# Top-k attention and SwiGLU FFN: a floor under the FFN pieces of even turns, and a slightly smaller share for the others

## The chip, the cores and the metric

The kernel runs on one core of a Trainium2 chip. The metric is the device time of one execution in microseconds; the time before is the median of three runs. The core's engines work through their own instruction queues in order: TensorE (PE in the profile, its weight loads PEld), VectorE (DVE), ScalarE (ACT), GpSimd (POOL), and SyncE (SP), whose queue issues nearly all of the transfers.

## What is computed

Attention with 8 batches, 8 heads, 576 positions and 64 numbers a head, in float32. Of each row of scores only the 32 largest count. The result, as 4608 tokens of 512 numbers, goes through a SwiGLU feed-forward network (FFN) with an inner width of 1536.

```python
scores = scale * np.matmul(q, k.transpose(0, 1, 3, 2))
kth = np.partition(scores, -top_k, axis=-1)[..., -top_k:-top_k + 1]
scores = np.where(scores >= kth, scores, -1000000000.0)
attn = np.exp(scores - np.max(scores, axis=-1, keepdims=True))
attn = attn / (np.sum(attn, axis=-1, keepdims=True) + 1e-09)
x = np.matmul(attn, v)               # then (B,H,S,D) -> (B*S, H*D)
g = x @ w_gate
out = (g * (1.0 / (1.0 + np.exp(-g))) * (x @ w_val)) @ w_out
```

## The kernel before

**Units.** Attention is cut into 160 units. A batch has 20 of them: five tiles of queries (`qt` 0 to 4), each for four pairs of heads (`hp` 0 to 3). The first four tiles have 128 queries and two heads each: full units. The fifth has the last 64 queries, and a unit of it holds both heads in one set of 128 rows, so it has one row block to select from instead of two: a short unit. Units 16 to 19 of every batch are short, so are units 36 to 39, 56 to 59, and so on.

**What a unit goes through.** `scores` multiplies queries and keys on PE into PSUM banks of the ring `ps_t` (five banks), and ACT copies them to `sc` (L314 for short units, L329 for full ones). `select` finds the 32 largest on DVE with four rounds of MAX8 (L346) and three of MATCH_REPLACE8 (L350). `shift` makes a bias on POOL (L361). `weigh` applies Prelu (L373) and Exp (L378) on ACT. `normalize` adds and inverts the sum on DVE (L391, L392) and scales `e`: from unit 12 on the first head on ACT (L396), the second, where there is one, on POOL (L398). `turn` transposes `e` on PE (`etps`, L411; nine transposes for a full unit, five for a short one) into banks of the same ring, and ACT copies them to `et` (L412). `values` multiplies with `v` on PE (`av`, L447), and ACT copies the result to `xT` (L463). `prep` transposes the keys and queries of the next batch on PE (`kqps`, L263 and L270), during the short turns and the first turn behind them.

**Turns.** The main loop runs over turns n. Turn n selects in unit n, weighs and scales unit n - 1, and transposes unit n - 2. Even turns also have the values of units n - 4 and n - 3 and the scores of units n + 1 and n + 2; odd turns have neither. (The scores of two short units are made together.) The order within a turn is written out by hand, and every engine keeps it, because at the end of the program each instruction is tied behind the one before it on its engine:

```python
        if nxt and (n < 2 or len(nxt) > 1):
            run(nxt.pop(0))          # scores of unit n + 1
        if valued(n):
            finish_units(valued(n))  # values
        ...                          # scores of unit n + 2, weigh(n - 1)
        pieces(2)
        flush(on_act)
        ...
            run(turn(n - TURN))      # transposes
        ...
        pieces(1)
        pieces(1)
        run(norm)
        ...
        pieces(6)
```

**Pieces.** The FFN runs over 18 blocks of 256 tokens. `feed` is a generator for one block, cut into pieces for PE. The first half of a block has 24 pieces of four matmuls (L591, tile `f`), each of a cost of 1 credit: two pieces fill a bank with a gate, two with a value, and each bank is then read by ACT (L624 to L626, or L631) and multiplied on POOL (L627, L632). The second half has seven quarters (L657, tiles `y_ps` and `x_ps`) of two pieces each, of 0.75 credit. It multiplies with sums and differences of weights and of halves of the block, which POOL makes (L664, L672, L677, L705); POOL also adds the results up (L644). The quarters run in the order i = 1, 7, 5, 6, 2, 4, 3. A block can start when attention has completed its tokens.

**Credit.** `share(n)` says how many credits a turn gets: 5.8 (turns below 32) or 6.4 (from turn 32 on, `AHEAD`) for a full unit and half of that for a short one, less what PE has else to do in the turn (0.7 for each unit of values and of scores, 0.6 for the transposes, half for short units, and 0.6 where keys and queries are prepared). In the loop, `credit[0] = min(credit[0] + share(n), share(n) + 1)`, and a call of `pieces(k)` takes up to k pieces while the credit is 1 or more. In the last four turns and the three behind them the credit is set to 8. What is left of the FFN comes behind the loop. The credit and the order decide only where a piece stands, not how many there are.

Of the kernel before, what the change touches and what calls it, by code (L numbers as in the profile page):

```python
# [25 lines left out]
def kernel(  # L26
# [49 lines left out]
    AHEAD = 8 * NHP  # L76
# [203 lines left out]
    units = [(b, qt, hp) for b in range(B) for qt in range(J + 1) for hp in range(NHP)]  # L280
    state = {}

    def n_heads(qt):

        return 1 if qt == J else 2
# [514 lines left out]
    def share(n):  # L800


        others = 0.0
        for m, cost in [(m, 0.7) for m in valued(n)] + [(n - TURN, 0.6)]:
            if m >= 0:
                others += cost * (0.5 if units[m][1] == J else 1)
        others += 0.7 * len(scored(n))
        if units[n + 3][1] == 0:
            others += 0.6

        beside = 5.8 if n < AHEAD else 6.4
        return beside * n_heads(units[n][1]) / 2 - others

    def scored(n):

        ahead = [n + 1] if n < 2 else [] if n % 2 else [n + 1, n + 2]
        return [m for m in ahead if m < NU and (units[m][1] < J or m % 2 == 0)]

    def valued(n):

        behind = [] if n % 2 else [n - 4, n - 3]
        return [m for m in behind if 0 <= m < NU]
# [33 lines left out]
    for n in range(NU + 3):  # L856
# [15 lines left out]
        if n >= NU - NHP:  # L872
            credit[0] = 8.0
        else:
            credit[0] = min(credit[0] + share(n), share(n) + 1)
# [93 lines left out]
```

## Time and profile before

| what | value |
|---|---|
| median of three runs | 1743.95 us (1743.23 to 1744.68) |
| the profiled execution's own time | 1745.19 us |
| its span, first to last instruction | 1743.4 us |
| mean granted TensorE clock | 0.970 |
| a full even and odd turn together, 507.6 to 530.0 us | 22.40 us |
| end of the last selection on DVE | about 1655 us |

A row of a group names the line of the kernel, the engine, the operation and the tiles (written, then read). A row of waits reads: engine, line and tile that waited, then after the arrow the engine, line and tile that released it, the total in us, how often, and the longest. In a timeline the first two numbers are start and length in us, and a bracket at the end holds the idle time of the engine just before the row and what ended it. The ends of matmuls are modelled, so the start of one to the start of the next is the better measure of PE's pace.

### The profile page before, as it was taken

What the parts mean: (1) busy time and instruction counts of PE and PEld (TensorE: products, weight loads), DVE (VectorE), ACT (ScalarE), POOL (GpSimd) and SP (SyncE); (2) the same over time, 40 slices, a digit from 0 to 9 for tenths busy, and PEclk for the clock granted to TensorE, in tenths of its full rate; (3) what the DMA queues carried; (4) which work ended last, traced back from release to release, by engine and by line L of the source; (5) the groups of instructions that cost most, each with busy time, mean ns of one, the idle gap of its engine ahead of it and who ended that gap; (6) DMA issues with size and microseconds to landing.
All of it is one profiled execution on the core that took longest, in us unless ns stands there. A gap on an engine that the chain in (4) does not pass through costs nothing.

```text
span 1743.4 us, 31763 instructions
## 1 busy us (share of the span) xinstructions
PE 1661.9 (95%) x11408; PEld 1399.7 (80%) x11408; DVE 1476.0 (85%) x3311; ACT 1259.9 (72%) x2901; POOL 798.4 (46%) x914
## 2 busy tenths in 40 slices
PE   5678999999999999999999999999999999999999
PEld 3468598788888788887888888888888878888887
DVE  6999898999989799898999898898988978898300
ACT  7899787778767686767776777778777767676531
POOL 4798454343353425352535334443444433535334
PEclk6698999999999999999999999999999999999999
DMA  7442030003000120002100030000300020000000
GB/s 204 138 121 86 23 76 2 13 3 82 15 13 1 29 70 1 13 12 60 28 14 1 14 71 27 1 13 20 78 2 13 1 57 15 13 1 13 1 13 12
DMA packets 109309, 59.72 MB, mean 34 GB/s; under 512 B 88544, under 2 KB 96992, under 8 KB 109152
## 3 DMA queue, kind: packets, MB, share of 16 engines
q1 hardware_dynamic: 108016, 57.37, 12.6%
q8 instruction: 90, 1.47, 0.4%
q14 instruction: 67, 0.55, 0.1%
q10 hardware_dynamic: 1136, 0.33, 0.1%
HBM read 48.23 MB, written 9.44 MB: 33 GB/s over the span
## 4 chain that ended last, share of the span: by engine, by line
PE 82%; DVE 7%; ACT 6%; POOL 2%; issue 1%; SPq 1%; DMA 0%; ACTq 0%; POOLq 0%
PE f L591 38%; PE av L447 9%; PE x_ps L657 9%; PE s L324 7%; PE etps L411 7%; PE y_ps L657 6%; DVE m L346 3%; DVE e L350 3%; PE f L507 2%; ACT e L378 2%; PE kqps L270 1%; PE o_ps L559 1%; DVE size L123 1%; ACT e L373 1%; POOL p L644 1%
## 5 line engine op out<-in xcount | busy, mean ns | idle before, releaser
L346 DVE MAX8 m<-e 128x8 f32<-128x576 f32 x864 | 614.6, 747 | 3.1
L350 DVE MATCH_REPLACE8 e<-m,e 128x576 f32<-128x576 f32 x576 | 423.6, 742 | 0.0
L591 PE MATMUL f<-xT,wg 128*128 128x256 f32 x1536 | 356.2, 382 | 0.0
L591 PE MATMUL f<-xT,wv 128*128 128x256 f32 x1536 | 355.2, 381 | 0.0
L591 PEld LDWEIGHTS f<-xT,wg 128*128 128x128 f32 x1536 | 288.5, 191 | 46.5 <-issue 8.8
L591 PEld LDWEIGHTS f<-xT,wv 128*128 128x128 f32 x1536 | 287.4, 190 | 42.9 <-issue 5.5
L627 POOL TENSOR_TENSOR h<-h,half_g 128x512 f32<-128x512 f32 x96 | 122.4, 1275 | 355.5 <-ACT h L626 339.6
L378 ACT ACTIVATE e<-e,bias 128x576 f32<-128x576 f32 x288 | 221.6, 779 | 37.3 <-POOL bias L361 34.3
L411 PE MATMUL etps<-ident,e 128*128 128x128 f32 x1312 | 183.5, 280 | 57.3 <-POOL e L398 25.0
L411 PEld LDWEIGHTS etps<-ident,e 128*128 128x128 f32 x1312 | 154.9, 143 | 86.6 <-POOL e L398 31.2
L373 ACT ACTIVATE e<-sc,m 128x576 f32<-128x576 f32 x288 | 212.4, 792 | 0.0
L350 DVE MATCH_REPLACE8 e<-m,sc 128x576 f32<-128x576 f32 x288 | 211.8, 742 | 0.0
L346 DVE MAX8 m<-sc 128x8 f32<-128x576 f32 x288 | 203.2, 742 | 7.0 <-ACT sc L329 7.0
L329 ACT ACTIVATE sc<-s 128x288 f32<-128x288 f32 x512 | 167.8, 418 | 53.8 <-PE s L324 53.4
L632 POOL TENSOR_TENSOR h<-h,val 128x512 f32<-128x512 f32 x96 | 122.4, 1275 | 173.4 <-ACT val L631 163.2
L398 POOL TENSOR_TENSOR e<-e,tot 128x576 f32<-128x576 f32 x140 | 160.6, 1151 | 81.5 <-DVE tot L392 72.2
L412 ACT COPY et<-etps 128x512 f32<-128x512 f32 (+1 forms) x448 | 184.6, 493 | 15.4 <-PE etps L411 14.9
L324 PE MATMUL s<-kqT 64*128 64x288 f32 x1024 | 172.5, 447 | 12.5 <-ACT et L412 5.9
L391 DVE TENSOR_SCALAR tot<-tot 128x1 f32<-128x1 f32 x228 | 29.3, 145 | 161.6 <-ACT e L378 161.5
L447 PE MATMUL av<-et,v 128*64 128x128 f32 (+1 forms) x2560 | 158.9, 268 | 0.0
L396 ACT ACTIVATE e<-e,tot 128x576 f32<-128x576 f32 x148 | 119.5, 807 | 49.3 <-DVE tot L392 48.9
L447 PEld LDWEIGHTS av<-et,v 128*64 128x64 f32 x2560 | 138.8, 141 | 5.9 <-issue 3.0
(86 smaller groups left out, 2216.8 us busy)
## 6 DMA issues: line engine op xcount, KB each, us to landing
v<-in_v_dram SPq DMA_DIRECT2D x32, 256.0 KB, 3.3
kq_in<-in_k_dram SPq DMA_DIRECT2D x63, 128.0 KB, 2.9
kq_in<-in_q_dram SPq DMA_DIRECT2D x63, 128.0 KB, 3.2
w<-in_moe_w_gate_dram SPq DMA_DIRECT2D x12, 512.0 KB, 3.8
w<-in_moe_w_val_dram SPq DMA_DIRECT2D x12, 512.0 KB, 3.7
w<-in_moe_w_out_dram SPq DMA_DIRECT2D x12, 512.0 KB, 3.6
out_dram<-o SPq DMA_DIRECT2D x38, 128.0 KB, 2.4
out_dram<-o SPq DMA_DIRECT2D x16, 256.0 KB, 2.4
```

Of the source, the lines that this page charges most:

```text
L324: nc.tensor.matmul(ps[:, 0:half], slab[d, q0 : q0 + P], slab[d, k0 : k0 + half])
L329: nc.scalar.mul(sc[:, i * half : (i + 1) * half], ps[:, 0:half], scale)
L346: nc.vector.max(m[:, t, 8 * r : 8 * r + 8], cur[:, hs])
L350: nc.vector.match_replace(e[:, hs], m[:, t, 8 * r : 8 * r + 8], cur[:, from_[t]], LOWEST)
L373: nc.scalar.activation(e[:, hs], sc[:, at], AF.Prelu, bias=m[:, t, TOP_K - 1 : TOP_K], scale=-1.0, alpha=SMALL,)
L378: nc.scalar.activation(e[:, hs], e[:, hs], AF.Exp, bias=bias[:, t : t + 1], scale=-1.0 / SMALL, accum_out=tot[:, t : t + 1],)
L398: nc.gpsimd.tensor_tensor(e[:, hs], e[:, hs], tot[:, t : t + 1].to_broadcast([P, S]), ALU.mult)
L411: nc.tensor.transpose(ps[:, c * P : (c + 1) * P], e[:, k0 : k0 + P], ident[:])
L412: nc.scalar.copy(et[:, c0 : c0 + cn, :], ps[:, 0 : cn * P].rearrange("p (c j) -> p c j", c=cn),)
L447: nc.tensor.matmul(av[d, i, 0:ql], weights_, moving, start=c == (0 if last else J), stop=c == (J if last else J - 1),)
L591: nc.tensor.matmul(ps[:, i, :], w[:, kc, m * P : (m + 1) * P], x[:, kc, :], start=(kc == 0), stop=(kc == KC - 1),)
L657: nc.tensor.matmul(ps, lhsT, T[i][m], start=m == 0, stop=m == MQ - 1)
```

## The change

From turn 32 on, `share` starts from 6.25 instead of 6.4 credits (3.125 instead of 3.2 for a short unit), and in even turns it returns no less than 2.0. The only even turns whose share lay below 2.0 are those of short units. Since `pieces(2)` is the first call in a turn, behind the scores and the values and ahead of the transposes, two pieces can then stand there in such turns.

```diff
         if units[n + 3][1] == 0:
             others += 0.6

-        beside = 5.8 if n < AHEAD else 6.4
-        return beside * n_heads(units[n][1]) / 2 - others
+        beside = 5.8 if n < AHEAD else 6.25
+        least = 2.0 if n >= AHEAD and n % 2 == 0 else 0.0
+        return max(least, beside * n_heads(units[n][1]) / 2 - others)
```

## The prediction

> **What bounds the kernel now.** I read the page from the top: busy shares, the chain of work that ended last, and then, for the part of the span that the change can reach (after 330 us), the waits of PE and a stretch of two pairs of full turns.
>
> ```profile
> span 1743.4 us, 31763 instructions
> PE 1661.9 (95%) x11408; PEld 1399.7 (80%) x11408; DVE 1476.0 (85%) x3311; ACT 1259.9 (72%) x2901; POOL 798.4 (46%) x914
> ...
> PE 82%; DVE 7%; ACT 6%; POOL 2%; issue 1%; SPq 1%; DMA 0%; ACTq 0%; POOLq 0%
> ```
>
> PE carries 82% of the chain. The windows view asks whether that holds in the steady part; its columns are the window, its length, then busy us of PE, PEld, DVE, ACT, POOL, the granted clock, DMA share and GB/s:
>
> ```profile
> 507.60:530.00 22.40, 22.40 (x148) 19.03 (x147) 20.91 (x49) 17.41 (x41) 7.66 (x8) 1.00 0.11 25
> 530.00:552.40 22.40, 22.40 (x148) 19.03 (x147) 20.04 (x47) 16.94 (x38) 8.93 (x9) 1.00 0.01 1
> ```
>
> An even and an odd full turn take 22.40 us, PE is busy in all of it, and DVE has 1.5 to 2.4 us to spare. So a full pair is bound by PE, and the whole time is PE's work plus PE's pauses. PE's waits from 330 to 1700 us:
>
> ```profile
> PE etps L411 <- ACT sc L314: 7.4, 6, 2.0
> PE etps L411 <- POOL e L398: 6.5, 4, 3.4
> PE etps L411 <- ACT e L396: 2.6, 1, 2.6
> PE etps L411 <- ACT sc L329: 2.5, 3, 1.1
> PE s L324 <- ACT et L412: 0.3, 1, 0.3
> ```
>
> Only 19 us of pauses are left, all but 0.3 at the transposes (etps). The two rows with sc, 9.9 us in nine places, are all in even turns of short units (turns 36, 56, 58, 76, 96, 98, 116, 118, 136). One of them, turn 56, in PE's timeline:
>
> ```profile
> 590.76 1.20 PE L307 MATMUL s<-kqT 64*64 64x288 f32 x16
> 591.89 0.66 PE L411 MATMUL etps<-ident,e 128*128 128x128 f32 x4
> 594.54 0.87 PE L411 MATMUL etps<-ident,e 128*128 128x128 f32 x5 [1.99 <-ACT sc L314]
> 595.24 2.72 PE L657 MATMUL x_ps<-wo,h 128*128 128x256 f32 x6
> ```
>
> The fifth transpose opens a second PSUM bank of the ring of five (ps_t). That bank still holds scores, and ACT copies scores out only behind the Prelu and Exp of the unit before (594.00 us). No FFN piece stands between the scores and the transposes, because the turn's credit is below 1.
>
> The POOL row is four odd turns (129, 137, 147, 155). In the worst, POOL's scaling of e for the second head stood behind an FFN block's sums:
>
> ```profile
> 1408.99 1.29 POOL L644 TENSOR_TENSOR p<-p,p 128x512 f32<-128x512 f32 x1
> 1410.21 2.11 POOL L705 TENSOR_TENSOR h<-h,xT 128x256 f32<-128x256 f32 x3
> 1412.26 1.17 POOL L398 TENSOR_TENSOR e<-e,tot 128x576 f32<-128x576 f32 x1
> ```
>
> **What a pause costs.** More than its length. The piece of turn 96 between two sets of transposes (nine transposes and f x16) takes 6.81 us with a pause of 2.00; at the rates of undisturbed turns (0.109 us a transpose, 0.216 an f instruction) it is 4.44. So a pause costs about 0.37 us above its modelled length. And the clock drops behind some:
>
> ```profile
> 595.30:598.70 3.40, 3.40 (x10) 2.66 (x10) 3.20 (x7) 3.31 (x8) 0.67 (x2) 0.50 0.02 5
> 800.10:803.40 3.30, 3.30 (x9) 2.60 (x9) 3.10 (x7) 3.21 (x8) 0.36 (x2) 0.50 0.00 0
> 1001.00:1004.40 3.40, 1.41 (x10) 1.15 (x9) 1.76 (x6) 3.40 (x12) 1.15 (x1) 1.00 0.00 0
> 1414.50:1417.80 3.30, 3.30 (x27) 2.94 (x27) 3.09 (x8) 3.30 (x9) 0.92 (x2) 0.50 0.18 41
> ```
>
> Behind the pauses at 592.55 (1.99 us), 797.01 (2.00) and 1410.07 (3.41) the granted clock is 0.50 for about 3.4 us, a loss of 1.7 us of PE each; behind the one at 1001.14 (2.00) it stays 1.00. The Trainium skill ("TensorE: Matmul & The Clock Gate", HAM oscillation) has the rule that PE must have no idle gap over about 3.4 us. By it only the third would lose clock, and my sum would be 3.4 us smaller. The rows show two losses behind 2 us, so I count three.
>
> **The change, part by part.** A piece is four matmuls, eight PE instructions in the trace, 8 x 0.216 = 1.73 us; in the second half of a block it is six of them, 1.30 us, and costs 0.75 of credit. A block is 24 + 14 x 0.75 = 34.5 credits.
>
> *Short even turns.* The share was 3.2 - 1.4 - 0.6 - 0.7 = 0.5 in the first and 0.2 in the third short turn; it becomes 2.0. Carrying share and credit through turn by turn, the first group of pieces, ahead of the transposes, got 0 or 1 in the twelve such turns from 36 to 138 and now gets 2 in every one; four of them also get a third piece behind the transposes. Two pieces are 2.6 to 3.46 us. The bank comes free 2.6 us after the last score matmul (591.9 to 594.5), so they just cover the wait. Of the first short turns, 36, 116 and 136, which already had one piece, pause 0.28 to 0.62 us; 56, 76 and 96, which had none, pause 2.0. Removed: 9.93 us of pauses, nine times 0.37 = 3.3, and two clock losses, 3.4: **16.6 us**.
>
> *What moves with a piece.* Every second piece brings ACT the reading of its bank, 0.60 + 0.60 + 0.64 us for a gate (L624 to L626) or 0.59 for a value (L631), and POOL a product of 1.28. These now stand ahead of the copies of et on ACT, so those, the kqT copies and the scaling of e for the next turn come later. In turn 58 of before the scaling ended 3.42 us behind the last transpose and was needed at 4.79; with a gate ahead it is about 4.6 against 4.4 to 4.8. I take 0.5 us in each of six odd short turns: **+3 us** (bounds 0, and +11 if the 1.83 us of a gate fell in full on all six). The loads of k and q on SP (L228, L233) wait for the transposes of kq_in, which come up to 5 us later, and stores queue behind them; the next use of such a tile is two turns, some 15 us, later, and a load lands in about 3 us: nothing. If that cover went, 3 us a batch.
>
> *Other turns.* 6.25 for 6.4 takes 0.15 credit from each full turn and 0.075 from an odd short one. A full pair has 8.5 credits for 8.8, so 22.40 - 0.3 x 1.73 = 21.88 us on PE, still above DVE's 20.04 to 20.91. Per batch of 20 turns the share goes from 76.8 to 77.56. PE's total is unchanged; what is done earlier is missing later.
>
> *Where blocks fall.* A block took 34.5 / 3.84 = 8.98 turns and takes 34.5 / 3.878 = 8.90; one is completed by attention every 160 / 18 = 8.89. So blocks used to drift against the turns and now keep step. The POOL burst above starts with a block's fifth quarter (i = 2). Carried through, that quarter started ahead of POOL's scaling in an even turn with full units in blocks 9, 12, 13, 14 and 15 (turns 102, 128, 136, 146, 154): the last four are the four waits. With the change it starts in an odd turn in every block from 3 to 15 but 11, whose turn 118 scales one head, on ACT. Behind an odd turn the next transposes are some 8 us off. Removed: 6.48 us, four times 0.37 = 1.5, one clock loss 1.7: **9.7 us**. What newly falls into even turns is the third quarter with its three subtractions (L677, 3 x 0.73); in turn 54 of before that put POOL's end 3.56 us behind the last transpose, needed at 4.4 at the least: nothing.
>
> *The tail.* By turn 158 three credits more are done, so turn 159 has 3.75 instead of 6.75 and the last unit's chain starts 5.2 us nearer. Its selection had then been waiting 12.65 us (DVE L391 at 1674.81), so it is not late. 30 pieces remain behind the loop as before, and the 2.62 us pause at 1673.5 stays.
>
> Sum: 16.6 + 9.7 - 3 = 23.3 us. The profiled execution took 1745.19 us (span 1743.4 and 1.8 around it), 1.24 above the median; 1745.19 - 23.3 - 1.24 = **1720.6 us**.
>
> **The rivals.**
>
> *Waits of POOL stay or come elsewhere.* Keeping step is as good or bad as the phase it keeps. If another burst meets the scaling, only the short turns gain: 1743.95 - 16.6 + 3 = 1730. Against: the phases above; for: margins of about 1 us at the third quarter.
>
> *DVE binds the full turns: slower.* The skill's page "Perfetto Trace Analysis" (Identifying the Most-Contended Engine) says that [...]weight loads tell the headroom. By these PE is at 19.03 / 22.40 = 85%, and DVE with 20.91 would be the bound. Then the smaller shares give nothing back, while the short turns pay 3.3 credits x 1.73 = 5.7 us a batch against 2.8 of removed waits: 6 x 2.9 = 17 slower, 5.2 back in the tail, 1756. It decides once a pair of DVE needs over 21.88 us. Against: PE's instructions follow at 0.216 us with no pause and DVE idles about 2.3 us in most even turns, so I take the row, not the rule.
>
> *The wait only moves.* Two pieces end and ACT, with the pieces' own reading, is late for the next transposes by as much: 1743 to 1741. The +11 us bound above is half of it. That the change does not do what it says is excluded by the credits: all twelve turns get their two.
>
> **How the numbers follow.** About 0.2%, 3.5 us, can be told from no change. Both kinds of wait go: 0.60 (1716 to 1725). Only the short turns' go: 0.22 (1725 to 1733). Gain smaller but over 3.5 us: 0.05. Within 0.2%: 0.05. Slower: 0.08. The range 1715 to 1733 leaves out the last three and a little of the first.
>
> **What would show it.** Right: no PE wait on ACT sc at etps after 330 us, POOL e at most 2 us, the granted clock at 0.50 nowhere between 330 and 1600 us, full pairs of 21.4 to 22.4 us with PE full, PE's busy time down by the clock losses. Wrong: waits PE etps on ACT e L396 or POOL e of over 5 us, DVE without idle time in even turns, or PE pauses before turn 160.

## The result, and the profile after

The changed kernel takes 1724.4 us (median of four runs, 1721.19 to 1724.58) where the kernel before takes 1743.59 (four runs): 0.9885 of it, with a 95% interval of 0.9868 to 0.9902. That is 19.2 us less; 23.3 were forecast, and 1724.4 lies in the range given. The profiled executions stand at 1724.45 and 1745.19 us.

The page of the changed kernel, with the lines that match those shown of before:

```profile
span 1722.7 us, 31765 instructions
PE 1654.3 (96%) x11408; PEld 1396.9 (81%) x11408; DVE 1476.5 (86%) x3311; ACT 1261.0 (73%) x2901; POOL 799.1 (46%) x914
...
PE 86%; DVE 6%; ACT 5%; issue 1%; POOL 1%; SPq 1%; DMA 1%; ACTq 0%; POOLq 0%
```

The same number of matmuls fills more of a shorter span. Who PE waited for from 330 to 1700 us (waited, released by, total us, times, longest):

```profile
PE etps L411 <- ACT e L396: 2.6, 1, 2.6
PE s L324 <- ACT et L412: 1.9, 5, 0.7
```

The rows on ACT sc (9.9 us before) and on POOL e (6.5) are gone. The one pause of the tail stays, and one row has grown: scores that wait for the copy of et, five times instead of once. Turn 56, the one shown of before, on PE:

```profile
589.80 1.20 PE L307 MATMUL s<-kqT 64*64 64x288 f32 x16
590.93 1.56 PE L657 MATMUL x_ps<-wo,h 128*128 128x256 f32 x6
592.33 1.89 PE L591 MATMUL f<-xT,wg 128*128 128x256 f32 x8
594.05 1.15 PE L411 MATMUL etps<-ident,e 128*128 128x128 f32 x9
```

Two pieces stand between the scores and the transposes, and the nine transposes run in one go, with no bracket for idle time behind them. A pair of full turns is bound by PE as before: two stretches of 22.40 us have PE full and leave DVE 1.9 and 2.4 us.

```profile
510.00:532.40 22.40, 22.40 (x148) 19.03 (x147) 20.48 (x47) 17.11 (x38) 8.19 (x9) 1.00 0.11 25
532.40:554.80 22.40, 22.40 (x148) 19.03 (x147) 20.04 (x47) 16.85 (x40) 7.96 (x9) 1.00 0.00 1
```

Where the time went, between the first transposes of turns 34, 156 and 160 in the two traces:

| stretch | before | after | difference |
|---|---|---|---|
| start to turn 34 | 374.16 | 374.26 | +0.1 |
| turn 34 to 156 | 1242.38 | 1225.44 | -16.9 |
| turn 156 to 160 | 56.22 | 51.04 | -5.2 |
| turn 160 to the end | 70.64 | 71.92 | +1.3 |

The changed kernel does three credits' worth of pieces, 5.2 us, more before turn 156 and as much less behind it. So the pauses between turns 34 and 156 shrank by 16.9 + 5.2 = 22.1 us.

### The profile page after: what moved, and what is told of

Same layout as the page of the kernel before. It is cut to its first block, busy times and chain, and to the rows that moved or that the text cites. A ratio compares the mean times of both kernels' runs of the same rounds, so it can differ in the third digit from the quotient of the medians.

```text
span 1722.7 us, 31765 instructions
## 1 busy us (share of the span) xinstructions
PE 1654.3 (96%) x11408; PEld 1396.9 (81%) x11408; DVE 1476.5 (86%) x3311; ACT 1261.0 (73%) x2901; POOL 799.1 (46%) x914
## 4 chain that ended last, share of the span: by engine, by line
PE 86%; DVE 6%; ACT 5%; issue 1%; POOL 1%; SPq 1%; DMA 1%; ACTq 0%; POOLq 0%
PE f L591 38%; PE x_ps L657 10%; PE av L447 9%; PE s L324 8%; PE y_ps L657 7%; PE etps L411 7%; PE f L507 3%; DVE m L346 3%; DVE e L350 2%; ACT e L378 1%; PE o_ps L559 1%; PE s L307 1%; PE kqps L270 1%; DVE size L123 1%; ACT et L412 1%
## 5 line engine op out<-in xcount | busy, mean ns | idle before, releaser
L591 PE MATMUL f<-xT,wv 128*128 128x256 f32 x1536 | 350.4, 379 | 0.0
L591 PEld LDWEIGHTS f<-xT,wv 128*128 128x128 f32 x1536 | 288.1, 190 | 39.4 <-issue 2.1
L411 PE MATMUL etps<-ident,e 128*128 128x128 f32 x1312 | 180.0, 280 | 40.9 <-POOL e L398 18.6
L324 PEld LDWEIGHTS s<-kqT 64*128 64x128 f32 x1024 | 95.7, 191 | 62.5 <-issue 24.2
```

The costliest lines, as they stand in the source:

```text
L324: nc.tensor.matmul(ps[:, 0:half], slab[d, q0 : q0 + P], slab[d, k0 : k0 + half])
L411: nc.tensor.transpose(ps[:, c * P : (c + 1) * P], e[:, k0 : k0 + P], ident[:])
L591: nc.tensor.matmul(ps[:, i, :], w[:, kc, m * P : (m + 1) * P], x[:, kc, :], start=(kc == 0), stop=(kc == KC - 1),)
```

## The experiments

Below, "lost" is the time between the first transposes of one turn and those of the next, less its instructions at the rates of undisturbed turns (0.109 us a transpose, 0.216 an f instruction, and so on). It holds a pause, its restart and a slow clock. From turn 34 to 160, 39.4 us were lost before and 17.2 after.

The theory: the change removes two kinds of waits. The floor puts pieces under the wait for a bank of scores; the new rate of credits keeps blocks in step with turns, which takes POOL's burst out of the turns where it hurts. The main rival: only the floor matters, or only the amount of work in the short turns.

**The floor alone** (e1_floor_only).

```diff
-        beside = 5.8 if n < AHEAD else 6.25
+        beside = 5.8 if n < AHEAD else 6.4
```

> The floor of 2.0 alone, the share left at 6.4. My theory: every short even turn still has its two pieces, so the waits of PE on ACT sc at the transposes are gone (16.6 us). But a batch then has 80.1 credits for 77.6 that attention supplies: blocks start as soon as they can, and 7, 4, 9, 9 and 4 calls in turns 65, 73, 109, 145 and 153 find no piece. Carried through, a block's fifth quarter starts ahead of POOL's scaling in even turns of full units six times (turns 54, 64, 90, 100, 126, 134), so POOL waits of 0.5 to 3.4 us come back, about 12 us with what follows them: 1735 to 1745. Rival (floor is all that counts, the smaller share is only a correction): as fast as the changed kernel, 1720 to 1726, with no POOL waits.

Measured: 1738.95 us, 0.9968 (0.9955 to 0.9981) of before.

```profile
PE etps L411 <- POOL e L398: 7.5, 5, 2.4
PE s L324 <- ACT sc L329: 3.1, 3, 1.2
```

No transposes wait for ACT sc, but five wait for POOL, in turns 55, 65, 91, 127 and 135: one turn behind five of the six even turns named. The sixth, 100, scales a short unit, which has no head on POOL. Behind the transposes of turns 109 and 145, where nine calls were counted to find no piece, the next scores wait 1.2 us each. Most of the floor's gain is lost again without the smaller share.

**The smaller share alone** (e2_share_only), the kernel before with 6.25 for 6.4.

> The share of 6.25 alone, without the floor. My theory: short even turns have 0 or 1 pieces, so nine to twelve waits on ACT sc stay; a batch has 74.1 credits, blocks lag, and the fifth quarter falls ahead of POOL's scaling in five even turns of full units (56, 104, 112, 142, 150): no gain, 1740 to 1750. Rival (smaller shares help the full turns by themselves): 1725 to 1735.

Measured: 1752.51 us, 1.0044 (1.0029 to 1.0059) of before: slower, and 2.5 us outside my expectation.

```profile
PE etps L411 <- ACT sc L314: 7.8, 6, 2.0
PE etps L411 <- POOL e L398: 7.2, 3, 3.4
PE etps L411 <- ACT sc L329: 2.0, 3, 0.7
PE x_ps L657 <- POOL h L705: 1.9, 2, 1.0
```

The short turns wait as before. POOL's burst is met by the transposes behind three of the five turns named (in 57, 105 and 113); in the other two (142 and 150) the next quarter on PE itself waits for the burst (L705, 0.9 and 1.0 us), which I had not counted. Smaller shares help nothing by themselves.

**The rate alone** (e3_rate_only): no floor, but as many credits a batch as after the change.

```diff
-        beside = 5.8 if n < AHEAD else 6.4
+        beside = 5.8 if n < AHEAD else 6.442
```

> No floor, but a share of 6.442, which gives a batch the 77.56 credits of the changed kernel. My theory of blocks keeping step: the fifth quarter starts in an odd turn in every block, so all waits of PE on POOL e after 330 us go (9.7 us), while the waits on ACT sc in short even turns stay at about 10 us: 1732 to 1736. Rival (the POOL waits went because the short turns became longer, not because of the phase): POOL waits of 5 us or more stay and the time is 1741 to 1746.

Measured: 1733.43 us, 0.993 (0.9914 to 0.9947), 11.4 us less than before and as expected.

```profile
PE etps L411 <- ACT sc L314: 4.3, 6, 2.0
PE etps L411 <- ACT sc L329: 2.9, 4, 1.0
PE etps L411 <- ACT e L396: 2.6, 1, 2.6
```

No row on POOL e is left, with the short turns nearly as poor in pieces as before (seven stand ahead of the transposes in the twelve turns, six before, 24 in the changed kernel). So 0.042 in the share was worth 11.4 us, because of where it makes blocks fall; but not all of that is POOL's. By the turns, the four POOL waits give 9.0 us. The short even turns lose 13.0 us instead of 17.0, since their pieces stand in other turns and one drop of the clock fewer follows. Some 3 us go to new waits behind ACT's copies (turns 57, 79, 97, 99 and 137).

**The place** (e4_behind): the changed kernel's credits, with the first two pieces of short even turns behind the transposes.

```diff
-        pieces(2)
+        behind = AHEAD <= n < NU - NHP and n % 2 == 0 and units[n][1] == J
+        if not behind:
+            pieces(2)
...
             run(turn(n - TURN))
+        if behind:
+            pieces(2)
```

> The changed kernel, with the first two pieces of the twelve short even turns taken behind the transposes instead of ahead of them; credits and blocks are the same. My theory (the place matters): waits on ACT sc of about 2.0 us come back in turns 36, 56, ..., 136 and of about 1 us in turns 38, 58, ..., 138, 18 us in the rows and up to 25 us with the restart and the clock: 1740 to 1750, with no POOL waits. Rival (the amount matters, the extra pieces fill the time wherever they stand): 1721 to 1727.

Measured: 1749.33 us, 1.0022 (1.0012 to 1.0032) of before.

```profile
PE etps L411 <- ACT sc L314: 10.0, 5, 2.1
PE etps L411 <- ACT sc L329: 4.0, 6, 0.7
PE s L324 <- ACT et L412: 3.9, 5, 1.3
```

The same pieces a few instructions later fill nothing: all the waits of short even turns are back (that of turn 36, 2.3 us, is put down to POOL h L672, though its transposes too go on when ACT has copied the first scores), and the whole gain is gone. The place decides, not the amount. The rival that the wait only moves falls as well, but for the 3.5 us shown below: ahead of the transposes the pieces take it away.

**POOL's burst** (e5_act_heads): the kernel before, with four scalings taken from POOL.

```diff
-            if t == 0 and n >= 3 * NHP:
+            if (t == 0 or n in (127, 135, 145, 153)) and n >= 3 * NHP:
```

> The kernel before, with the second head of units 127, 135, 145 and 153 scaled on ACT instead of POOL (the four units whose transposes waited for POOL). My theory: the POOL waits in turns 129, 137, 147 and 155 and the clock drop at 1414 us are gone, 9.7 us less up to 2 us for ACT's four extra scalings: 1734 to 1738. Rival (PE's wait only moves, since ACT is the next to be late): 1741 to 1745 with waits on ACT e in the same turns.

Measured: 1740.22 us, 0.9967 (0.9954 to 0.998): 5.7 us less, not 8 to 12 (4.4 up to turn 156 in the profiles; the tail happened to keep its full clock in this one). In three of the four turns nothing is left. In turn 137 the wait moved a few instructions down (this kernel's timeline, in order of time):

```profile
1409.33 2.11 POOL L705 TENSOR_TENSOR h<-h,xT 128x256 f32<-128x256 f32 x3
...
1411.39 0.19 POOL L361 TENSOR_TENSOR bias<-m 128x1 f32<-128x1 f32 x1
1411.62 0.77 ACT L378 ACTIVATE e<-e,bias 128x576 f32<-128x576 f32 x1 [1.96 <-POOL bias L361]
...
1412.64 1.24 ACT L412 COPY et<-etps 128x512 f32<-128x512 f32 x3
...
1413.28 0.33 PE L263 MATMUL kqps<-ident,kq_last 128*128 128x128 f32 x1 [2.59 <-ACT et L412]
```

The burst also holds up the next unit's bias (0.19 us of POOL), ACT's Exp waits for the bias, and the copies of et wait behind the Exp. So both theories hold a part: three waits were POOL's scaling, the largest was the burst in two ways. The clock also still drops there. In the run of the rate alone the burst is out of this turn and both waits are gone (what is left there, 0.5 us, is for a gate read by ACT).

**What the changed kernel still loses: the fourth short turn.** Turns 59, 79, 99, 119 and 139 lose 6.5 us together (3.0 before). Turn 59 in the changed kernel's timeline:

```profile
612.56 0.57 ACT L624 ACTIVATE h<-f 128x512 f32<-128x512 f32 x1
612.70 0.71 PE L411 MATMUL etps<-ident,e 128*128 128x128 f32 x5
613.04 0.58 ACT L625 ACTIVATE half_g<-f 128x512 f32<-128x512 f32 x1
...
613.52 0.63 ACT L626 ACTIVATE h<-h 128x512 f32<-128x512 f32 x1
...
614.04 0.75 ACT L412 COPY et<-etps 128x512 f32<-128x512 f32 x2
...
614.66 1.10 ACT L275 COPY kqT<-kqps 128x512 f32<-128x512 f32 x2
614.67 1.89 PE L324 MATMUL s<-kqT 64*128 64x288 f32 x8 [0.28 <-ACT et L412]
```

The copy of et stands behind the reading of a gate, and the scores need its bank; all eight then take 1.89 us, against 1.24 in an undisturbed turn. Turn 139 is the same; in 79 and 99 a value is read there (L631).

Turn 119 has the longest of the five waits, 0.72 us, and another cause: POOL's burst once more. The fifth quarter of block 11 starts in turn 118, as the prediction had counted, and the burst stands ahead of the next unit's bias:

```profile
1215.20 2.10 POOL L705 TENSOR_TENSOR h<-h,xT 128x256 f32<-128x256 f32 x3
1217.26 0.19 POOL L361 TENSOR_TENSOR bias<-m 128x1 f32<-128x1 f32 x1
1217.48 0.78 ACT L378 ACTIVATE e<-e,bias 128x576 f32<-128x576 f32 x1 [2.34 <-POOL bias L361]
...
1218.50 0.75 ACT L412 COPY et<-etps 128x512 f32<-128x512 f32 x2
...
1219.14 1.89 PE L324 MATMUL s<-kqT 64*128 64x288 f32 x8 [0.72 <-ACT et L412]
```

This is the chain of turn 137 in the run above: burst, bias, Exp, copy of et. DVE is not the cause, as I took it to be ahead of the next run: its last MAX8 for this unit ended at 1210.2 us, 7 us before the bias.

For the other four, my first cure was to read the gate or value later (e6_flush_late):

```diff
-        flush(on_act)
+        late = AHEAD <= n < NU - NHP and n % 2 == 1 and units[n][1] == J
+        if not late:
+            flush(on_act)
...
             run(turn(n - TURN))
+        if late:
+            flush(on_act)
```

> The changed kernel, with ACT's reading of finished FFN banks put behind the transposes, and so behind the copies of et, in the odd short turns. The changed kernel lost 6.5 us at PE s on ACT et in turns 59, 79, 99, 119 and 139 (3.0 before). If it is the reading of the gate on ACT that holds up the copy of et, the four waits of about 1.2 us in 59, 79, 99 and 139 go and 119 stays (its Exp waits for a bias from DVE): 3 to 4 us less than the changed kernel. Rival (the scores wait for the copies of kqT or for DVE in any case): no difference, within 1 us.

Measured: 1724.73 us, 0.9878 (0.9863 to 0.9893): no different from the changed kernel. The theory fell:

```profile
PE s L324 <- ACT kqT L275: 2.5, 4, 1.0
PE s L324 <- ACT et L412: 0.4, 1, 0.4
```

The same scores now wait for the copies of kqT, which the reading had pushed back instead. In these four turns it is ACT's whole queue that is late, in whatever order. The row on et is turn 119, which waits for POOL as before.

The second cure leaves ACT alone and gives PE something to do (e9_third_piece): one more piece in that turn, ahead of the next scores, and 0.05 less in the share elsewhere, so that a batch keeps 77.5 credits.

```diff
-        beside = 5.8 if n < AHEAD else 6.25
+        beside = 5.8 if n < AHEAD else 6.2
         least = 2.0 if n >= AHEAD and n % 2 == 0 else 0.0
+        if fourth(n):        # AHEAD <= n < NU - NHP, qt == J, hp == NHP - 1
+            least = 3.0
...
         next(ahead, None)
-        pieces(1)
+        if not fourth(n):
+            pieces(1)
         next(ahead, None)
```

> The changed kernel with a floor of 3.0 in the fourth short turn of each batch (39, 59, ..., 139), whose third piece stands behind the transposes of keys and queries and ahead of the next turn's scores; the other shares go from 6.25 to 6.2, so that a batch keeps 77.5 credits and blocks keep step. My theory: the wait of the scores there is for ACT's chain of copies (et, then kqT) to end, whatever their order, and 1.3 to 1.7 us of PE work in front of it covers it: most of the 6.5 us lost in these turns goes, 4 to 6 us less than the changed kernel. Rival (ACT is the bound of these turns, so that the wait comes one step later): within 1.5 us of it.

Measured: 1718.63 us, 0.985 (0.9836 to 0.9863). The changed kernel, run again beside it:

> The changed kernel once more beside the two, on the same chip: 0.9885 of the kernel before. If the half clock behind the last wait lasts 3.4 instead of 6.8 us, the tail is 1.7 us shorter.

It took 1721.47 us, 0.9869 (0.9855 to 0.9882). From turn 34 to the end the two profiles differ by 4.4 us (1342.4 and 1346.8), inside the 4 to 6 expected; the medians, which hold the start too, by 2.8. All five waits are gone, that of turn 119 too: in this run the burst comes behind the bias of that turn (bias at 1207.70 us, burst from 1212.44). The smaller share was not run by itself. The waits of the third piece's kernel from 330 to 1700 us:

```profile
PE etps L411 <- ACT e L396: 2.6, 1, 2.6
PE kqps L263 <- ACT et L412: 0.3, 1, 0.3
```

**The tail** (e7_tail6): a credit of 6 instead of 8 in the last turns.

```diff
         if n >= NU - NHP:
-            credit[0] = 8.0
+            credit[0] = 6.0
```

> The changed kernel, with a credit of 6 instead of 8 in the last turns. Then turn 160 still has six pieces of 0.75, four of them between the last two sets of transposes. My theory: the wait of 2.61 us at 1651.5 us (PE etps on ACT e) is filled, and with it goes the half clock of 6.8 us behind it: 2.6 + 0.4 + 3.4 = 6 us less than the changed kernel. Rival (the last unit's chain is only pushed later by the pieces, so nothing is won): within 1.5 us of the changed kernel.

Measured: 1720.08 us, 0.9851 (0.9836 to 0.9866). The pause of 2.61 us and the half clock behind it are gone. From turn 34 to the end its profile has 1343.7 us against 1348.4 and 1346.8 in the two profiles of the changed kernel, 4.7 and 3.1 less. The second, the repeated run of the changed kernel, had only 3.4 us of half clock, for which 2.6 + 0.4 + 1.7 = 4.7 would be expected; some 1.6 us are missing. The records of PE from turn 156 on show where they went. In the repeated run pause, restart and half clock cost 4.1 us together, since the half clock began 0.4 us before the pause was over. And with a credit of 6 the quarters of the tail lose 0.9 us more, at short waits for POOL (L664, 0.18 us in turn 158; L705, 0.06 us in turn 160) and their restarts.

With the later reading of the gate as well (e8_both):

> The changed kernel with both edits, the reading behind the transposes in odd short turns and a credit of 6 in the last turns: the sum of the two, 8 to 10 us less than the changed kernel, 1714 to 1717.

Measured: 1721.88 us, 0.986 (0.9844 to 0.9877): no better than the tail alone, since the later reading gives nothing. With the third piece as well (e10_third_tail6):

> The same with a credit of 6 in the last turns, which by itself gave 4 to 5 us: the sum, 8 to 10 us less than the changed kernel, about 1715. If the two share a cause, no better than 1720.

Measured: 1716.32 us, 0.983 (0.9817 to 0.9843), the fastest here, 5.2 us below the changed kernel on the same chip, with 0.5 us of PE waits left between 330 and 1700 us. Its profile has 1339.0 us from turn 34 on, 7.8 less than that of the repeated run: close to the sum of the two gains in the profiles, 4.4 and 3.1. The medians show less of it, because the first 374 us differ by 1 to 2 us from run to run.

## Why the prediction was right, point by point

*PE binds, so removed pauses count in full.* Right. 22.1 us fewer were lost up to turn 156, and all of it came off the end but for 1.3 us more in the tail. The rival of DVE as the bound had the measure of weight loads at its side that the Trainium skill names ("Perfetto Trace Analysis", Identifying the Most-Contended Engine). It falls: PE is full in both stretches with weight loads at 85%. The twelve full turns from turn 44, 64, 84, 104 and 124 on take 126 to 130 us (128 to 129 before) without a pause of PE, and DVE is busy in 91 to 92% of them, 19.4 to 19.6 us a pair, under the 21.88 at which it would decide. Single pairs vary from 19.4 to 22.8 us with the pieces in them, more than the 21.4 to 22.4 given; their mean is 21.4.

*Short even turns, 16.6 us.* Right in size and place: the turns named lost 17.0 us before and no more than an undisturbed turn after. The run with the pieces behind the transposes shows that it is the place.

*Blocks keep step, 9.7 us.* Right in the main: the four turns lost 9.0 us more before than after, no transposes wait for POOL in the changed kernel, the run of the rate alone shows the same without the floor, and rates that drift (floor alone, share alone) bring the waits back, mostly in the turns counted out. What the step did not see is the second way of the burst, through the bias. In turn 137 it made no odds, since both ways vanish with the burst. But block 11, whose burst was counted as harmless because turn 118 scales one head, on ACT, met the bias in turn 119. That it cost only 0.4 us more than in the other fourth short turns was luck, as nothing in the prediction bounded it.

*What moves with a piece, +3 us.* The size was right, the place not, so the size was in part luck. I expected waits of transposes on ACT's scaling of e. It was the scores of the next turn that waited for the copies of et, and for kqT behind them, in the fourth short turn: 3.5 us more than before in five turns, of which turn 119, 1.3 us, is the burst's. Three odd turns (57, 77, 97) lost 0.1 to 0.2 us more each.

*The tail, 0.* The pause stayed at 2.61 us, as said, but the half clock behind it lasted 6.8 us in this profile, 3.4 in that of before (why is shown in the last section):

```profile
1653.50:1660.30 6.80, 6.18 (x51) 5.29 (x52) 0.00 (x0) 1.58 (x4) 0.00 (x0) 0.50 0.24 55
```

That is the +1.3 us; in the repeated run it was 3.4 us again and the tail 70.4 us. The three credits missing in turn 159 cost nothing, as forecast: turns 156 to 160 are shorter by 5.2 us, the three credits' own work.

*The sum.* The forecast was 1720.6 us, 3.8 less than measured. Of these, 1.2 are in the steady part (22.1 us of loss removed for 23.3), 1.3 in the tail and 0.1 ahead of turn 34. The other 1.2 were taken off because the profiled execution of before was slower than its median by that much; that of the changed kernel lies at its median.

*The other rivals.* "The wait only moves" came true for one term alone, at 3.5 us with turn 119 in it. Of the signs named ahead, these showed: no wait on ACT sc or POOL e, no half clock between 330 and 1600 us, PE's busy time down (by 7.6 us).

## What to carry to other kernels

Where one engine is full, look at its few pauses one by one: what ended each, and which work of that engine could stand in front of it without changing what it has to do. A piece of work hides a wait only at its own place in the queue; the same piece a few instructions later is worth nothing. And in a schedule run by credits, compare the rate at which work is handed out with the rate at which it arrives: when the two differ, the pattern drifts until two bursts meet, and a change of a few hundredths in a share can move 10 us.

## What the runs showed that was not expected

The granted clock fell to 0.50 for 3.4 us behind pauses of PE of only 2 us, and not behind every one. In the profiles of before, e1, e2, e3, e4 and e5, between 330 and 1600 us, 21 pauses of 1.99 to 2.36 us stand, and 12 of them are followed by a drop, 1.7 us of PE each. So such a pause costs on average 2.0 + 0.4 + 1.0 us.

The traces tell which ones. In each of the thirteen profiles every stretch of half clock starts at a multiple of 3.413 us from the first one (in before, 595.28 and 800.08 us are 60 such steps apart). What counts is how much of a pause lies in one step:

| run, start of the pause | length, us | in one step, in the next | half clock behind it |
|---|---|---|---|
| before, 592.55 | 1.99 | 1.99 | 3.4 us |
| before, 1001.14 | 2.00 | 0.33, 1.67 | none |
| before, 1509.52 | 2.14 | 0.53, 1.61 | none |
| e3, 594.84 | 1.99 | 0.09, 1.91 | 3.4 us |
| e5, 1668.88 | 2.62 | 1.31, 1.30 | none |
| changed kernel again, 1652.22 | 2.61 | 2.18, 0.44 | 3.4 us |
| changed kernel, 1651.50 | 2.61 | 2.02, 0.59 | 6.8 us |

Of all pauses of over 0.9 us between 330 and 1700 us in the thirteen profiles, the 23 with 1.91 us or more in one step all have a drop, and the 25 with 1.73 us or less have none. The half clock lasted a second step in the two cases with 0.59 and 0.67 us of the pause left in the next step, and not in the two with 0.28 and 0.44. So the length of a pause does not tell its price: one of 2.6 us cost no clock where the steps cut it in half, and the same pause of the tail cost 3.4 or 6.8 us of half clock in two profiles of one kernel.
